# Nyström attention with a folded feed-forward: v loaded in four gated pieces, q and k in halves between sums, batch 1 loaded ahead of the weights

## Chip, cores and metric

The kernel runs on one core of one Trainium2 chip. The metric is the device time of one execution in microseconds (us), as the median of several runs. Before the change it is 294.45 us, the median of 8 runs that lie between 293.55 and 297.5.

## What is computed

```python
# attention, for each of 8 batches x 8 heads, seq 576, head_dim 64, m = 32 landmarks
q_lm = q.reshape(B, H, m, S // m, D).mean(axis=3)      # k_lm likewise
A = sm(q, k_lm);  Bm = sm(q_lm, k_lm);  C = sm(q_lm, k)
Z = Bm.T / (norm1(Bm) * norminf(Bm) + 1e-06)
for _ in range(6):
    Z = 2 * Z - Z @ Bm @ Z
attn = A @ Z @ C @ v
# feed-forward on x = attn as (4608 tokens, 512)
h = (x @ w1) * (x @ w2) @ w3
out = h @ w_out
```

`sm` is the softmax of the scaled product. w1 and w2 are 512 x 1024, w3 is 1024 x 1024, w_out is 1024 x 512, all fp32.

## The kernel before

**The algebra.** The kernel multiplies w3 and w_out once into w34 (the fold). Per batch it never forms x: it multiplies the small attention factors into w1 and w2 (tile `gt`, L403 to L419), and the large matmuls are `up` (L422), which multiplies `gt` by the normalised scores `ahat` for eight units j and both weights, and `down` (L439), which multiplies their product `ab` by w34 and stores 128 rows at a time. An even batch has four down chunks, an odd one five.

**One batch's attention** (`attention`, L178) is a generator. Each `yield` ends a step, and the main loop calls `steps(at)` to place one step between two pieces of matmul work. Step 1 turns landmark sums into the tile `lm` (L183 on TensorE, L188 on ScalarE, `qbd` on VectorE). Then come the small scores (L199), the scores of C with their partial sums on GpSimd (`presum`, L235 to L240), `bmn` and `bmbd` on GpSimd (L259, L262), the scores of A (L274), two steps `cv` that read v (L305), six Newton iterations (L369), the normalisation (L353) and four steps that make `gt` (L412, which is the first reader of w1 and w2).

**Loads of a batch.** `load_qk` (L68) issues two transfers on GpSimd's queue, k and then q, cast to fp16, into `qkn`. `turn_all` (L512) issues four DMA transposes on SP's queue, two for k and two for q, from `qkn` into `qkT`. `landmarks` (L158) adds up groups of the transposed k (t = 1) or q (t = 0) with six GpSimd operations, L166 to L175, into `parts`, which step 1 of the attention reads. `load_v` (L75) is one transfer on SP's queue. `qkn`, `qkT` and `vt` have two buffers each. Batch 0 is turned on TensorE instead (`turn_on_pe`, L94), with one copy on ScalarE and one on VectorE.

**The front** (L522 to L602). `fold` (L464) is a generator with 64 steps. Step n is three matmuls (L489) of a row block of w3 with a slice of w_out; between them it turns half blocks of w3 (L476), turn(j, 1) at step 8j and turn(j+1, 0) at step 8j+5 for j from 2 on. w3 arrives in blocks 0 to 7 on SP's queue (`load_w3`, L527) into three buffers. GpSimd's queue has k and q of batch 0, then w1 and w2 in four transfers. The order of the rest is written out by hand. Two small GpSimd copies (L572, L578) act as gates: they write one element of the buffer that a load is going to fill, and read `qkn`, so the load on SP can't start before the q or k that they read is there. After 33 fold steps the loop of L589 places attention 0 between the other fold steps, and within it the loads and landmark sums of batch 1.

**The main loop** (L607 to L636). Batch b runs its eight units of `up` and its chunks of `down`; between them are the steps of attention b+1, and at the end step 1 of attention b+2. In the same pass the transposes and v of batch b+2 are issued at the start, and after the ups q and k of batch b+3 are issued and batch b+2's landmarks are summed. Batch 0 has a schedule of its own: attention 1 begins only in its third unit, and its later downs take two steps each.

Each engine executes its instructions in the order in which the program emits them, so a queue holds everything behind an instruction that waits.

Of the kernel before, what the change touches and what calls it, by code (L numbers as in the profile page):

```python
# [7 lines left out]
FP32 = mybir.dt.float32  # L8
FP16 = mybir.dt.float16
# [4 lines left out]
B = 8  # L14
H = 8
# [10 lines left out]
NP = 96  # L26
# [5 lines left out]
def kernel(  # L32
# [11 lines left out]
    nc = tc.nc  # L44
    consts = ctx.enter_context(tc.tile_pool(name="consts", bufs=1))
    wpool = ctx.enter_context(tc.tile_pool(name="wpool", bufs=1))
    pin = ctx.enter_context(tc.tile_pool(name="pin", bufs=2))
# [5 lines left out]
    def big():  # L53
        return psp.tile([128, 2, 512], FP32, name="big", bufs=3)
# [13 lines left out]
    def load_qk(st, b):  # L68
        qkn = pin.tile([128, 2, H, 384], FP16, name="qkn")
        for t, src in ((1, k), (0, q)):  # L70
            nc.gpsimd.dma_start(out=qkn[0:NP, t, :, :],
                                in_=src[b].rearrange("h (p r) d -> p h (r d)", p=NP))
        st["qkn"] = qkn

    def load_v(st, b):  # L75
        vt = st["vt"] if "vt" in st else pin.tile([128, H, 384], FP32, name="vt")
        nc.sync.dma_start(out=vt[0:NP], in_=v[b].rearrange("h (p r) d -> p h (r d)", p=NP))
        st["vt"] = vt

    def load_weight(t, w):  # L80
        for qd in range(2):
            nc.gpsimd.dma_start(out=wup[64 * qd:64 * qd + 64, :, t, :],
                                in_=w[256 * qd:256 * qd + 256, :].rearrange("(h d) j -> d h j", d=D))
# [10 lines left out]
    def turn_on_pe(st, t, h0, copy):  # L94
        if "qkT" not in st:
            st["qkT"] = pat.tile([128, 2, H, 3, NP], FP16, name="qkT")
        ps = psp.tile([128, 2, 1024], FP16, name="big", bufs=3)
        for i in range(2):
            for n in range(6):
                nc.tensor.transpose(  # L100
                    out=ps[:, i, NP * n:NP * n + NP],
                    in_=st["qkn"][0:NP, t, h0 + 2 * i + n // 3, 128 * (n % 3):128 * (n % 3) + 128],
                    identity=ident16[0:NP, 0:NP])
        copy(out=st["qkT"][:, t, h0:h0 + 4, :, :].rearrange("p (i h) c s -> p i (h c s)", i=2),
             in_=ps[:, :, 0:6 * NP])
# [49 lines left out]
        return mask4, par, ones, eye2, iit, onesq, selc, lomask  # L155


    def landmarks(st, t, eng=nc.gpsimd):  # L158
        if "parts" not in st:
            st["parts"] = pz.tile([128, 2, 2, H, 32], FP16, name="parts")  # L160
        for h0 in ((0,) if eng is nc.gpsimd else (0, 4)):
            own, n = ("", H) if eng is nc.gpsimd else ("v", 4)
            hs = slice(h0, h0 + n)
            x = st["qkT"][:, t, hs, :, :]
            tr = pat.tile([128, n, NP], FP32, name="tr" + own, bufs=1)
            eng.tensor_tensor(out=tr, in0=x[:, :, 0, :], in1=x[:, :, 1, :], op=ALU.add)  # L166
            eng.tensor_tensor(out=tr, in0=tr, in1=x[:, :, 2, :], op=ALU.add)  # L167
            t3 = tr.rearrange("p h (l g) -> p h l g", g=3)
            o = pat.tile([128, n, 32], FP32, name="o3" + own, bufs=1)
            hi, lo = st["parts"][:, 0, t, hs, :], st["parts"][:, 1, t, hs, :]  # L170
            eng.tensor_tensor(out=o, in0=t3[:, :, :, 0], in1=t3[:, :, :, 1], op=ALU.add)
            eng.tensor_tensor(out=o, in0=o, in1=t3[:, :, :, 2], op=ALU.add)  # L172

            eng.tensor_copy(out=hi, in_=o)
            eng.tensor_tensor(out=lo, in0=o, in1=hi, op=ALU.subtract)  # L175


    def attention(st, bank=None):  # L178
# [331 lines left out]
    sts = [dict() for _ in range(B)]  # L510

    def turn_all(b):  # L512
        for t in (1, 0):
            for h0 in (0, 4):
                transposes(sts[b], t, range(h0, h0 + 4))

    def steps(g, n=1):
        for _ in range(n):
            next(g, None)
# [3 lines left out]
    with tc.tile_pool(name="pf", bufs=2) as pf:  # L523
        wof, w3f = {}, {}
        wsp = pf.tile([128, 2, 8, DM], FP16, name="wsp", bufs=1)

        def load_w3(j, cc=None, eng=nc.sync):  # L527
            if j not in w3f:
                w3f[j] = pf.tile([128, DF], FP32, name="w3f", bufs=3)
            sl = slice(0, DF) if cc is None else slice(512 * cc, 512 * cc + 512)  # L530
            eng.dma_start(out=w3f[j][:, sl], in_=moe_w3[128 * j:128 * (j + 1), sl])

        def load_wout(c, eng):
            wof[c] = pf.tile([128, DM], FP32, name="wof", bufs=6)
            eng.dma_start(out=wof[c], in_=moe_w_out[128 * c:128 * c + 128, :])

        load_w3(0, 0)
        load_wout(0, nc.scalar)
        load_wout(1, nc.sync)
        load_w3(1, 0, nc.scalar)  # L540
        load_wout(2, nc.sync)
        load_wout(3, nc.scalar)
        load_w3(0, 1)
        load_wout(4, nc.scalar)
        load_w3(1, 1)
        load_wout(5, nc.scalar)

        warm = pf.tile([128, 512], FP16, name="warm", bufs=1)
        nc.vector.memset(warm, 0.0)
        psw = big()  # L550

        def warm_up(n):
            for _ in range(n):
                nc.tensor.matmul(psw[:, 0, :], warm[:, 0:128], warm, start=True, stop=True)

        warm_up(7)

        nc.gpsimd.tensor_copy(out=gate, in_=wof[4][:, 0:1])
        load_qk(sts[0], 0)
        load_weight(0, moe_w1)  # L560
        load_weight(1, moe_w2)
        mask4, par, ones, eye2, iit, onesq, selc, lomask = constants()
        fd = fold(pf, wof, w3f, wsp, warm_up)
        steps(fd, 1)
        load_wout(6, nc.sync)
        load_wout(7, nc.sync)
        load_w3(2)
        steps(fd, 7)
        load_w3(3)
        steps(fd, 11)  # L570
        w3f[4] = pf.tile([128, DF], FP32, name="w3f", bufs=3)
        nc.gpsimd.tensor_copy(out=w3f[4][0:NP, 0:1], in_=sts[0]["qkn"][0:NP, 1, 0, 0:1])  # L572
        load_w3(4)
        turn_on_pe(sts[0], 1, 0, nc.scalar.copy)
        turn_on_pe(sts[0], 1, 4, nc.vector.tensor_copy)
        landmarks(sts[0], 1)
        sts[0]["vt"] = pin.tile([128, H, 384], FP32, name="vt")
        nc.gpsimd.tensor_copy(out=sts[0]["vt"][0:NP, 0, 0:1], in_=sts[0]["qkn"][0:NP, 0, 0, 0:1])  # L578
        load_v(sts[0], 0)
        load_qk(sts[1], 1)  # L580
        steps(fd, 5)
        turn_on_pe(sts[0], 0, 0, nc.scalar.copy)
        turn_on_pe(sts[0], 0, 4, nc.vector.tensor_copy)
        landmarks(sts[0], 0)
        steps(fd, 3)
        load_w3(5)
        steps(fd, 6)
        at = attention(sts[0])
        for n, m in enumerate((2, 2, 2, 2, 2, 2, 2, 1, 1, 1, 1, 1, 1, 1, 2, 2, 2, 2, 2, 1)):  # L589
            steps(at)  # L590
            if n == 3:
                load_w3(6)
            elif n == 7:
                load_w3(7)
                load_v(sts[1], 1)
                turn_all(1)
                landmarks(sts[1], 1)
                load_qk(sts[2], 2)
                landmarks(sts[1], 0)
            steps(fd, m)  # L600
        steps(at, 30)
        steps(fd, 64)  # L602
    pab = ctx.enter_context(tc.tile_pool(name="pab", bufs=3))
    at = attention(sts[1], acc)


    for b in range(B):  # L607
        st = sts[b]
        ab = st["ab"] = pab.tile([128, 8, S], FP16, name="ab")
        if b + 2 < B:  # L610
            turn_all(b + 2)
            load_v(sts[b + 2], b + 2)
        if b % 2 == 0:
            chunks = [[(b, ab, 128 * t, 128)] for t in range(4)]
        else:
            chunks = [[(b - 1, sts[b - 1]["ab"], 512, 64), (b, ab, 0, 64)]]
            chunks += [[(b, ab, 64 + 128 * t, 128)] for t in range(4)]
        for j in range(8):
            up(st, j, 0)
            steps(at, (0, 0, 1, 1, 1, 1, 1, 2)[j] if b == 0 else 1)  # L620
            up(st, j, 1)
        if b + 3 < B:
            load_qk(sts[b + 3], b + 3)
        if b + 2 < B:
            landmarks(sts[b + 2], 1)
            landmarks(sts[b + 2], 0)
        nxt = attention(sts[b + 2], acc) if b + 2 < B else iter(())
        hold = {}
        nd = 2 * len(chunks)
        for n in range(nd):  # L630
            bank = (lambda: big()[:, 0, :]) if n // 2 % 2 else acc
            down(chunks[n // 2], n % 2, hold, bank)
            steps(at, 2 if n == 6 and nd == 8 or b == 0 and n > 3 else 1)
        steps(at, 30)
        steps(nxt)
        at = nxt  # L636
# [30 lines left out]
```

## Time and profile before

| | |
|---|---|
| median of 8 runs | 294.45 us |
| the profiled execution's own time | 294.78 us |
| its span, first to last instruction | 292.7 us |
| TensorE (PE) busy | 276.1 us, 94% |
| VectorE (DVE) busy | 166.8 us, 57% |
| GpSimd (POOL) busy | 146.6 us, 50% |
| ScalarE (ACT) busy | 127.9 us, 44% |
| DMA | 45.56 MB, mean 156 GB/s |
| first `up` of batch 0 | 75.45 us after the start |

The page of the profile divides the span into equal slices, lists busy time per engine and the costliest groups of instructions by source line, and follows the chain of work that ended last. Further answers are taken from the trace: the waits of one engine by line and releaser, tables of busy time for chosen stretches, the instructions in order of time, and the transfers with the time from issue to landing. L12 is line 12 of the kernel before. SPq and POOLq are the instruction streams that issue transfers; PEld is TensorE's weight load. The granted clock is the share of full speed that TensorE had.

### The profile page before, as it was taken

The numbers are of one execution on the slowest core, as the hardware profiler recorded it, in microseconds if no ns is written. First come the engines' busy times: TensorE is split into PE (matmuls) and PEld (weight loads), VectorE is DVE, ScalarE is ACT, GpSimd is POOL, SyncE is SP. The second block draws the span as 40 slices with busy tenths as digits, with TensorE's granted clock in tenths as the row PEclk, the third lists the DMA queues.
The fourth block names the chain that finished last, engine by engine and source line by source line (L and its number), as shares of the span: only waits on it lengthen the run. The fifth ranks groups of instructions, "written<-read, shape, count | busy, mean of one in ns | idle before, by whom it ended". The sixth has DMA issues, their size and how long they took to land.

```text
span 292.7 us, 9468 instructions
## 1 busy us (share of the span) xinstructions
PE 276.1 (94%) x4028; PEld 151.5 (52%) x4028; DVE 166.8 (57%) x430; ACT 127.9 (44%) x207; POOL 146.6 (50%) x190
## 2 busy tenths in 40 slices
PE   8999878999999899999999999999999999999993
PEld 3456435543574366436644753376457435744741
DVE  7733223364475677647656765476666655665720
ACT  3635224224471374247426722572366246625531
POOL 1506916098069839923991698069809931500000
PEclk9999979999999999999999999999999999999999
DMA  7999999929969569947996999399959532012124
GB/s 252 282 240 243 211 271 258 155 50 175 168 148 133 142 141 163 210 140 139 167 210 173 163 206 195 79 171 215 203 127 157 129 102 72 4 36 76 37 56 123
DMA packets 61449, 45.56 MB, mean 156 GB/s; under 512 B 35040, under 2 KB 53472, under 8 KB 61408
## 3 DMA queue, kind: packets, MB, share of 16 engines
q1 hardware_dynamic: 47056, 32.12, 49.9%
q0 software_dynamic: 13632, 11.54, 25.4%
q10 hardware_dynamic: 720, 1.31, 1.3%
q8 instruction: 31, 0.51, 0.7%
q14 instruction: 10, 0.08, 0.1%
HBM read 38.80 MB, written 9.44 MB: 165 GB/s over the span
## 4 chain that ended last, share of the span: by engine, by line
PE 77%; DMA 6%; DVE 6%; ACT 6%; issue 2%; POOL 2%; SPq 0%; DVEq 0%; ACTq 0%; POOLq 0%
PE big L426 18%; PE acc L446 13%; PE big L446 11%; PE acc L489 8%; DMA w3f<-in_moe_w_dram 6%; PE big L412 6%; PE big L369 4%; DVE ab L432 4%; PE small L305 2%; ACT a_sb L430 2%; PE big L476 2%; PE acc L305 2%; PE small L489 2%; PE big L353 1%; PE big L274 1%
## 5 line engine op out<-in xcount | busy, mean ns | idle before, releaser
L426 PE MATMUL big<-ahat,gt 128*128 128x288 f16 x512 | 74.1, 286 | 2.8 <-ACT a_sb L430 1.7
L432 DVE TENSOR_TENSOR ab<-a_sb,big 128x576 f16<-128x576 f16 x64 | 48.0, 750 | 18.7 <-PE big L426 7.8
L426 PEld LDWEIGHTS <-gt 128*128 128x128 f16 x512 | 47.2, 98 | 19.3 <-issue 4.4
L430 ACT CAST a_sb<-big 128x576 f16<-128x576 f32 x64 | 40.9, 639 | 37.1 <-PE big L426 36.3
L235 POOL TENSOR_TENSOR t<-ect 96x384 f32<-96x384 f32 x16 | 15.9, 994 | 71.5 <-ACT ect L228 70.9
L489 PE MATMUL acc<-wsp,w3t 128*128 128x512 f16 x168 | 42.7, 388 | 0.5 <-ACT w L492 0.5
L446 PE MATMUL acc<-w,ab 128*128 128x512 f16 (+1 forms) x192 | 41.0, 382 | 0.1
L446 PEld LDWEIGHTS <-ab 128*128 128x128 f16 (+1 forms) x320 | 24.0, 100 | 32.7 <-issue 9.8
L446 PE MATMUL big<-w,ab 128*128 128x512 f16 x128 | 32.8, 381 | 0.2 <-DVE ahat L356 0.2
L166 POOL TENSOR_TENSOR tr<-qkT 128x768 f32<-128x768 f16 x16 | 26.3, 1643 | 12.1 <-DMA qkT<-qkn 7.2
L418 DVE TENSOR_SCALAR gt<-big 128x1024 f16<-128x1024 f32 x16 | 19.6, 1225 | 21.7 <-PE big L412 21.7
L489 PEld LDWEIGHTS <-w3t 128*128 128x128 f16 x192 | 18.0, 99 | 21.1 <-issue 4.4
L452 ACT ACTIVATE o_sb<-acc 128x512 f32<-128x512 f32 x20 | 11.9, 597 | 38.5 <-PE acc L446 36.7
L167 POOL TENSOR_TENSOR tr<-tr,qkT 128x768 f32<-128x768 f32 x16 | 26.3, 1641 | 1.3
L482 DVE SCALAR_TENSOR_TENSOR w3t<-big,w3t 128x512 f16<-128x512 f32 x16 | 11.0, 689 | 19.2 <-ACT w3t L481 19.2
L416 ACT ACTIVATE gt<-big 128x1024 f16<-128x1024 f32 x16 | 16.4, 1023 | 8.5 <-PE big L412 8.5
L412 PE MATMUL big<-wup,zt 64*32 64x512 f16 x512 | 19.3, 381 | 0.0
L452 ACT ACTIVATE o_sb<-big 128x512 f32<-128x512 f32 x16 | 9.6, 597 | 22.0 <-PE big L446 22.0
L481 ACT ACTIVATE w3t<-big 128x512 f16<-128x512 f32 x16 | 9.5, 595 | 12.5 <-PE big L476 9.4
L228 ACT ACTIVATE ect<-big 96x768 f32<-96x768 f32 x16 | 12.9, 806 | 3.6 <-PE big L224 3.1
L172 POOL TENSOR_TENSOR o<-o,tr 128x256 f32<-128x256 f32 x16 | 12.8, 799 | 1.3
L356 DVE TENSOR_TENSOR ahat<-eat,big 128x576 f16<-128x576 f16 x16 | 11.9, 748 | 1.2 <-PE big L353 1.2
(307 smaller groups left out, 355.3 us busy)
## 6 DMA issues: line engine op xcount, KB each, us to landing
vt<-in_v_dram SPq DMA_DIRECT2D x8, 1152.0 KB, 9.6
qkn<-in_k_dram POOLq DMA_DIRECT2D x8, 576.0 KB, 11.1
qkn<-in_q_dram POOLq DMA_DIRECT2D x8, 576.0 KB, 13.9
out_dram<-o_sb SPq DMA_DIRECT2D x24, 192.0 KB, 2.3
w3f<-in_moe_w_dram SPq DMA_DIRECT2D x6, 512.0 KB, 13.6
out_dram<-o_sb SPq DMA_DIRECT2D x24, 128.0 KB, 2.7
wup<-in_moe_w_dram POOLq DMA_DIRECT2D x4, 512.0 KB, 19.5
out_dram<-o_sb SPq DMA_DIRECT2D x24, 64.0 KB, 2.0
```

The source lines that it names most:

```text
L166: eng.tensor_tensor(out=tr, in0=x[:, :, 0, :], in1=x[:, :, 1, :], op=ALU.add)
L167: eng.tensor_tensor(out=tr, in0=tr, in1=x[:, :, 2, :], op=ALU.add)
L235: nc.gpsimd.tensor_tensor(out=t3[0:NP], in0=e[:, :, 0:3, :], in1=e[:, :, 3:6, :], op=ALU.add)
L412: nc.tensor.matmul(psG[32 * h:32 * h + 32, qd, :], zt[rs, i, h, :], wup[rs, h, w, fs], start=(i == 0), stop=(i == 1), tile_position=(64 * ...
L416: nc.scalar.activation(out=g[:, :, w, fs], in_=psG, func=AXF.Copy, scale=1.0 / ZS)
L418: nc.vector.tensor_scalar(out=g[:, :, w, fs], in0=psG, scalar1=1.0 / ZS, scalar2=None, op0=ALU.mult)
L426: nc.tensor.matmul(p[:, c, 0:HS], st["g"][:, qd, w, 128 * j:128 * j + 128], st["ahat"][qd][:, c, :], start=(qd == 0), stop=(qd == 1))
L430: nc.scalar.copy(out=st["a_sb"], in_=p[:, :, 0:HS])
L432: nc.vector.tensor_tensor(out=st["ab"][:, j, :].rearrange("p (c s) -> p c s", c=2), in0=st["a_sb"], in1=p[:, :, 0:HS], op=ALU.mult)
L446: nc.tensor.matmul(pso[o:o + sz, :], ab[:, j, s0:s0 + sz], w34[:, j, :], start=(j == 0), stop=(j == 7), tile_position=(0, o))
L452: nc.scalar.activation(out=o_sb, in_=pso[:, :], func=AXF.Copy, scale=1.0 / (X64 * X64))
L489: nc.tensor.matmul(psW[j][:, :], turned[j, c // 4][:, a, c % 4, :], wsp[:, b, c, :], start=(c == 0 and a + b == 0), stop=(c == 7 and a == 1))
```

## The change

The diff has three parts.

*In the main loop*, v of batch b+2 is no longer one load at the start of the pass. It becomes four pieces of two heads each, issued in units 4 to 7 on SP's queue. Each piece has a gate: a ScalarE copy of one column of the `a_sb` tile just made into the first element of the piece. q and k of batch b+3 become four transfers of four heads each, which GpSimd issues in the middle and at the end of each set of landmark sums instead of ahead of them. The sums are emitted after unit 5 instead of after unit 7.

*In the front*, q and k of batch 1 are issued on GpSimd's queue ahead of w1 and w2. k of batch 0 is turned after fold step 16 (before: 19) and q after step 21 (before: 24). The gate of v and its load come ahead of the k sums. Blocks 5 and 6 of w3 and batch 1's four transposes are emitted earlier; block 7 and v of batch 1 now follow the transposes on SP's queue. Attention 0 begins after 31 fold steps (before: 33).

*For batch 0*, step 1 of attention 1 is placed ahead of the main loop, and batch 0 then has one step per unit and per down, like the other even batches.

```diff
+    def load_v_piece(st, b, i, done):
+        if i == 0:
+            st["vt"] = pin.tile([128, H, 384], FP32, name="vt")
+        hs = slice(2 * i, 2 * i + 2)
+        nc.scalar.copy(out=st["vt"][0:NP, 2 * i, 0:1], in_=done)
+        nc.sync.dma_start(out=st["vt"][0:NP, hs],
+                          in_=v[b, hs].rearrange("h (p r) d -> p h (r d)", p=NP))
+
+    def qk_pieces(st, b):
+        st["qkn"] = pin.tile([128, 2, H, 384], FP16, name="qkn")
+        for t, src in ((1, k), (0, q)):
+            for i in range(2):
+                hs = slice(4 * i, 4 * i + 4)
+                nc.gpsimd.dma_start(out=st["qkn"][0:NP, t, hs, :],
+                                    in_=src[b, hs].rearrange("h (p r) d -> p h (r d)", p=NP))
+                yield
...
-    def landmarks(st, t, eng=nc.gpsimd):
+    def landmarks(st, t, eng=nc.gpsimd, pieces=iter(())):
...
             eng.tensor_tensor(out=tr, in0=tr, in1=x[:, :, 2, :], op=ALU.add)
+            next(pieces, None)
...
             eng.tensor_tensor(out=lo, in0=o, in1=hi, op=ALU.subtract)
+            next(pieces, None)
...
         load_qk(sts[0], 0)
+        load_qk(sts[1], 1)
         load_weight(0, moe_w1)
         load_weight(1, moe_w2)
...
-        steps(fd, 11)
+        steps(fd, 8)
         w3f[4] = pf.tile([128, DF], FP32, name="w3f", bufs=3)
         nc.gpsimd.tensor_copy(out=w3f[4][0:NP, 0:1], in_=sts[0]["qkn"][0:NP, 1, 0, 0:1])
         load_w3(4)
+        sts[0]["vt"] = pin.tile([128, H, 384], FP32, name="vt")
+        nc.gpsimd.tensor_copy(out=sts[0]["vt"][0:NP, 0, 0:1], in_=sts[0]["qkn"][0:NP, 0, 0, 0:1])
+        load_v(sts[0], 0)
         turn_on_pe(sts[0], 1, 0, nc.scalar.copy)
         turn_on_pe(sts[0], 1, 4, nc.vector.tensor_copy)
         landmarks(sts[0], 1)
-        sts[0]["vt"] = pin.tile([128, H, 384], FP32, name="vt")
-        nc.gpsimd.tensor_copy(out=sts[0]["vt"][0:NP, 0, 0:1], in_=sts[0]["qkn"][0:NP, 0, 0, 0:1])
-        load_v(sts[0], 0)
-        load_qk(sts[1], 1)
         steps(fd, 5)
         turn_on_pe(sts[0], 0, 0, nc.scalar.copy)
         turn_on_pe(sts[0], 0, 4, nc.vector.tensor_copy)
         landmarks(sts[0], 0)
-        steps(fd, 3)
         load_w3(5)
+        steps(fd, 4)
+        load_w3(6)
+        turn_all(1)
         steps(fd, 6)
         at = attention(sts[0])
         for n, m in enumerate((2, 2, 2, 2, 2, 2, 2, 1, 1, 1, 1, 1, 1, 1, 2, 2, 2, 2, 2, 1)):
             steps(at)
-            if n == 3:
-                load_w3(6)
-            elif n == 7:
+            if n == 1:
                 load_w3(7)
                 load_v(sts[1], 1)
-                turn_all(1)
+            elif n == 4:
                 landmarks(sts[1], 1)
                 load_qk(sts[2], 2)
                 landmarks(sts[1], 0)
...
     at = attention(sts[1], acc)
+    steps(at)
...
             turn_all(b + 2)
-            load_v(sts[b + 2], b + 2)
...
             up(st, j, 0)
-            steps(at, (0, 0, 1, 1, 1, 1, 1, 2)[j] if b == 0 else 1)
+            steps(at, 1)
+            if b + 2 < B and j > 3:
+                load_v_piece(sts[b + 2], b + 2, j - 4, st["a_sb"][0:NP, 0, 0:1])
             up(st, j, 1)
-        if b + 3 < B:
-            load_qk(sts[b + 3], b + 3)
-        if b + 2 < B:
-            landmarks(sts[b + 2], 1)
-            landmarks(sts[b + 2], 0)
+            if b + 2 < B and j == 5:
+                pieces = qk_pieces(sts[b + 3], b + 3) if b + 3 < B else iter(())
+                landmarks(sts[b + 2], 1, pieces=pieces)
+                landmarks(sts[b + 2], 0, pieces=pieces)
...
-            steps(at, 2 if n == 6 and nd == 8 or b == 0 and n > 3 else 1)
+            steps(at, 2 if n == 6 and nd == 8 else 1)
```

## The prediction

> **What bounds the kernel now.** I read the waits of TensorE first, then a table of stages, then the timeline of the front, and then the chain of waits. On the page PE is busy 94% of the span. All its waits for another engine or a transfer, largest first:
>
> ```profile
> PE small L183 <- POOL parts L174: 2.0, 1, 2.0
> PE big L426 <- ACT a_sb L430: 1.7, 8, 0.2
> PE big L476 <- DMA w3f<-in_moe_w_dram: 1.5, 2, 1.3
> ```
>
> The columns are us in total, times, longest. Two single waits, of 2.0 and 1.3 us, stand out, and both lie in the front, where w3 is folded with w_out. Everything later is many tiny ones. In the chain of waits the only transfer is that of w3f, 6% of the span. The stages (us, then PE, PEld, DVE, ACT and POOL busy, the granted clock, DMA share, GB/s):
>
> ```profile
> 35.39:38.10 2.71, 0.49 (x2) 0.10 (x2) 0.35 (x1) 0.00 (x0) 2.43 (x4) 0.88 1.14 222
> 38.10:44.47 6.37, 5.11 (x33) 2.18 (x33) 1.55 (x5) 1.61 (x3) 0.34 (x1) 0.78 1.13 287
> 75.45:104.28 28.83, 27.24 (x463) 15.26 (x461) 17.80 (x45) 14.03 (x24) 17.81 (x22) 1.00 0.68 135
> 133.45:160.02 26.57, 25.98 (x457) 14.83 (x457) 18.03 (x46) 13.06 (x22) 17.79 (x22) 1.00 0.99 178
> 189.79:216.41 26.62, 26.03 (x457) 14.88 (x458) 18.04 (x46) 13.07 (x22) 17.80 (x22) 1.00 0.92 177
> ```
>
> The first two rows are the front's hole: PE idles 2.22 us and then 1.26 us, and in between it runs at a reduced clock. The other three are the three even batches (0, 2, 4), which have the same work; batch 0 is 2.2 us longer. Odd batches carry one more down chunk and take 28.75 to 29.77.
>
> Why the hole is there shows in the front's timeline:
>
> ```profile
> 29.58 0.67 POOL L175 TENSOR_TENSOR parts<-o,parts 128x256 f16<-128x256 f32 x1
> 30.20 0.18 POOL L578 CAST vt<-qkn 96x1 f32<-96x1 f16 x1
> 30.32 0.82 POOL L71 DMA_DIRECT2D qkn<-in_k_dram  x1
> 30.40 0.33 SPq L77 DMA_DIRECT2D vt<-in_v_dram  x1
> 30.82 0.96 SPq L531 DMA_DIRECT2D w3f<-in_moe_w_dram  x2
> 31.12 0.78 POOL L71 DMA_DIRECT2D qkn<-in_q_dram  x1
> 31.90 1.66 POOL L166 TENSOR_TENSOR tr<-qkT 128x768 f32<-128x768 f16 x1
> ```
>
> GpSimd finishes the k sums (L175), only then makes the gate copy L578; SP, held at v (L77), only then gets to w3 blocks 5 and 6 (L531); block 5 lands 13.6 us after its issue, at 44.4. And GpSimd issues batch 1's loads (1.6 us) before the q sums (L166), for which PE waits at L183.
>
> **The front, step by step.** The k turn moves from fold step 19 to 16, the q turn from 24 to 21, attention's start from 33 to 31. One fold step is three matmuls, 0.65 us. PE reached turn(2,1) at 19.55; the k turn now stands there. It needs k, issued at 9.15 and landed 9.8 later, at 18.95: 0.6 us ahead. It ends at 20.7, and the sums start 0.95 later as before (L100's end 23.12, L166 at 24.07), at 21.7. But the v gate now stands ahead of them and needs q: 10.11 + 11.7 = 21.8, plus 0.18 is 22.0. That wait costs 0.3 us; queued behind it are only these sums. k sums take 6.18 (24.07 to 30.25), so 28.2; no load issue between; q sums 6.15, so 34.35, against 38.05 before. PE comes to L183 two fold steps (1.3) before its old 35.39, so at 34.1. The wait of 2.22 falls to about 0.2: **2.0 gained**.
>
> Clock: over 37.50 to 41.50 the granted clock was 0.58, so (1 - 0.58) x 4.0 = 1.7 us of PE work was lost. The Trainium skill (TensorE: Matmul & The Clock Gate, section Why this matters for your kernels) keeps full clock as long as no idle gap passes about 3 us. By that rule this hole, 1.96 + 0.26 idle, costs no clock and 0 is won; the row says it did cost. I take the row, since the slow stretch begins right there: **1.7 gained**.
>
> Block 5: SP now holds w3f[4] at 19.3, v at 22.0 (the gate), block 5 at about 22.5 instead of 30.82. With the same 13.6 us it lands at 36.1. PE wants it at 43.21 (end of work before the wait) - 2.0 - 1.7 + 1.02 (L248 0.33 and L224 0.69 now stand ahead of turn(5,0)) = 40.5. **1.26 gained**, with 4.4 us of cover.
>
> What else these moves push back: k and q of batch 1 (2.36 MB in HBM) now stand ahead of w1, w2 on POOL's queue. Before, the weights landed by about 35 (12.70 + 22.8) and are first read at L412, 65.95. Now batch 1 took 23.9 us in the worst of its rows beside SP's loads, so by 45.7; the weights took 14 us behind q: at worst 60, with w1, read first, by 53. L412 comes at 65.95 - 5.0 - 1.9 (two fold steps and a turn that now follow it) = 59, w2 a step later. Hidden, but thinly in the worst case. On SP, batch 1's four transposes now stand ahead of block 7. Before they followed it, waited for k and q (47.2, 55.0) and took 4.27, 3.48, 2.29 and 1.36 us to issue, 11.4 in all. If q lands between 34 and 45, block 7 is issued between 42 and 50 and lands 6 to 13.6 later: 48 to 64. PE wants it at 64.52 - 5.0 + 1.03 (L353, L412 now ahead) = 60.5. Middle 55: nothing; upper end 3 us of wait. The sums of batch 1 wait for the transposes, 52 to 56 plus 14, 66 to 70, against L183 at about 70: even.
>
> **Batch 0.** Attention 1 now starts ahead of the loop, and then gets one step per unit, as in batches 2 and 4. So batch 0 should take their 26.6 instead of 28.83; the two L183 matmuls (0.43) move in front: **1.8 gained**. Bounds: 0.7 (only the difference of the gaps, 1.6 against 0.6, less fills) and 2.2.
>
> **The steady batches.** In the built program GpSimd's arithmetic keeps its order: the two units sooner move nothing there, since presums and bmbd of the same batch are emitted before both places. Only the loads move. Four ScalarE copies (96x1) per batch, 24 in all, come between a_sb copies of units 4 to 7. Their cover:
>
> ```profile
> 142.09 0.64 ACT L430 CAST a_sb<-big 128x576 f16<-128x576 f32 x1 [0.98 <-PE big L426]
> 144.02 0.64 ACT L430 CAST a_sb<-big 128x576 f16<-128x576 f32 x1 [1.29 <-PE big L426]
> 145.59 0.64 ACT L430 CAST a_sb<-big 128x576 f16<-128x576 f32 x1 [0.93 <-PE big L426]
> ```
>
> ScalarE idles 0.93 to 1.29 us before each next a_sb, for PE. The nearest rows are GpSimd's gate, 0.18, and ScalarE's smallest copy, L203 at 0.22 to 0.26; a gate also waits for a_sb's end. Fully exposed it would be 24 x 0.26 = 6.2; within 0.9 us of idle I take 0. Its only transfer waits are for v two batches older, long landed. Behind a late gate stand the next a_sb, then DVE and PE.
>
> v comes later: last piece at a_sb of unit 7, 146.2 + 0.2; even with the whole load's 11.2 us it is there at 157.6, and L305 reads it at 166.7. q and k halves: issued 3.4 to about 15 us after bmbd instead of at once, the last at 155.3 to 156.9 (141.5 + 12.2 of sums + 1.6 to 3.2 of issue). Landing in 6 us (64.52 to 70.6) gives 162; SP wants it at the fourth transpose, 164.6. At the worst row, 13.9, the transposes slip 6 us, and the q sums still start after them. The sums end at 156.9 at most instead of 155.3; L183 comes at 158.7. The Trainium skill (DMA: Bandwidth & Descriptors, sections Measured and Anatomy of one DMA) speaks against pieces: at least 1 MiB per transfer, or bandwidth is lost, and some 2 us fixed for each; by that, 18 more transfers for v and 10 more for q and k are an estimated 56 us of queue. The rows say that a load of v took 9.6 us to land and is wanted some 25 us after issue; as PE waits for no v or qkn after 60 us, the rule prices cover, not time. I take 0; below it, up to -0.7 if the single 0.68 us issue gap at 176 is tied to v's burst.
>
> **Sum.** 2.0 + 1.7 + 1.26 + 1.8 = 6.8 us. The profiled execution took 294.78 (span 292.7 and 2.1 around it): 288.0. It lies 0.3 above the median, 294.45, so 287.7 of the median.
>
> **Rivals.**
> 1. *The front stays bound by transfers* (DMA share 1.08 to 1.14 up to 44 us, so nothing is moved faster): a block or the weights land 2 to 4 us late and the wait reappears at L476 or L412, perhaps with its slow clock. For it: the same bytes; against it: block 5 is issued 8 us sooner and has 4.4 us of cover. Time 290 to 292. Chance 0.14.
> 2. *The gates are exposed* by 0.2 each, 4.8, or batch 0 gains only 0.7 and half of the gates show: 292 to 294. Against it: the idle above. Chance 0.07.
> 3. *Slower: SP's order.* Block 7 stands behind transposes that wait for batch 1's q. From a landing after 60.5 every us counts; after 67.3 all is lost, and a long hole costs slow clock again. That needs q landed only at 52 or so: 52 + 4 + 13.6 = 69.6, 9 us late, less the 6.8: 296 to 298. For it: q of batch 1 landed at 55.0 before; against it: it was issued at 31.1 then, at about 12 now. Chance 0.06.
> 4. *What is said to be done isn't what acts:* the steady batches' edits do nothing for PE. That is in my forecast, not beside it.
>
> **Numbers.** Forecast (0.73): 286 to 290, likeliest 287.7. Range 285.8 to 291.8, which takes in most of rival 1. Half a per cent, 1.5 us, is about what can be told from no change: faster 0.87, same 0.07, slower 0.06.
>
> **What would show it.** PE's wait at L201 (old L183) under 0.3; no reduced clock after 35; no wait over 0.3 for w3f at L494 (old L476); batch 0 from its first up to batch 1's at 26.6; the start of batch 0 near 70.5; batches 1 to 7 within 0.3 us each; L84 copies at 0.18 to 0.26 without a PE wait for a_sb. Wrong, if a w3f or wup wait appears between 48 and 62, or if the even batches lengthen.

## Result and the profile after

The changed kernel takes 289.11 us, the median of 11 runs (288.07 to 291.79), beside 294.75 of 32 runs of the kernel before. The ratio is 0.982, with a 95% interval of 0.980 to 0.985: 4.4 to 5.9 us faster. (Medians here and below are of all runs; ratios leave out the runs that lie over 1.5% above the fastest of their kernel.) 287.7 was forecast. The profiled execution took 289.36, its span is 287.6 instead of 292.7, and the granted clock is 9 in all 40 slices of its page. Lines are now those of the kernel after: L183, L199, L412, L426, L476 and L489 of before are L201, L217, L430, L444, L494 and L507.

The waits of PE after, largest first (total, times, longest, in us):

```profile
PE acc L217 <- ACT lm L206: 1.7, 7, 0.3
PE big L444 <- ACT a_sb L448: 1.7, 8, 0.2
PE big L430 <- issue: 1.4, 1, 1.4
PE big L572 <- DVE warm L567: 1.2, 1, 1.2
PE acc L507 <- ACT w L510: 0.7, 3, 0.2
```

Both large waits of before are gone: of the wait for `parts` 0.14 is left, and the one wait for w3f (0.4) is for the very first block, at 4.6 us. In their place stands one single stall that was not there before, 1.4 at L430, for "issue", that is, for nothing the profile shows.

The timeline of GpSimd and SP shows why the two waits went:

```profile
21.23 0.18 POOL L594 CAST vt<-qkn 96x1 f32<-96x1 f16 x1 [2.71 <-DMA qkn<-in_q_dram]
21.68 1.64 POOL L183 TENSOR_TENSOR tr<-qkT 128x768 f32<-128x768 f16 x1 [0.26 <-DVE qkT L121]
...
27.80 1.64 POOL L183 TENSOR_TENSOR tr<-qkT 128x768 f32<-128x768 f16 x1
...
33.30 0.67 POOL L192 TENSOR_TENSOR parts<-o,parts 128x256 f16<-128x256 f32 x1
```

```profile
21.44 0.33 SPq L77 DMA_DIRECT2D vt<-in_v_dram  x1
21.87 6.78 SPq L549 DMA_DIRECT2D w3f<-in_moe_w_dram  x2
28.74 23.62 SPq L106 DMA_TRANSPOSE qkT<-qkn  x4
52.45 1.00 SPq L549 DMA_DIRECT2D w3f<-in_moe_w_dram  x1
```

The gate (L594) waits for q but costs the sums nothing (they start 0.26 after it, for the turn's copy). The two sets of sums follow each other with no load issue between, and the last ends at 33.97, with PE at L201 from 33.50. Block 5 is issued at 21.87 and lands 16.0 later, at 37.8; PE takes it at 40.43. Block 7 goes out at 52.45, behind transposes that hold SP for 23.62, and lands at 57.1; PE takes it at 60.69.

The stages, with the columns of the table of before (us; PE, PEld, DVE, ACT and POOL busy; clock, DMA share, GB/s):

```profile
35.42:41.00 5.58, 5.33 (x55) 3.38 (x54) 2.48 (x9) 2.14 (x5) 1.39 (x2) 1.00 1.15 256
72.96:100.42 27.46, 26.63 (x461) 15.12 (x459) 18.16 (x46) 14.60 (x28) 18.91 (x24) 1.00 0.63 125
100.42:129.52 29.10, 28.11 (x472) 15.52 (x473) 18.09 (x47) 14.18 (x27) 18.86 (x24) 1.00 0.92 170
129.52:156.09 26.57, 25.98 (x456) 14.83 (x457) 18.03 (x46) 13.71 (x26) 18.89 (x24) 1.00 0.95 175
156.09:184.85 28.76, 28.06 (x474) 15.45 (x474) 18.15 (x47) 14.19 (x27) 18.91 (x24) 1.00 0.90 171
```

Two rows of before that stand against these, the slow stretch and batch 3, and the stall of PE inside batch 3:

```profile
37.50:41.50 4.00, 3.74 (x18) 1.15 (x17) 0.69 (x1) 0.74 (x2) 0.54 (x1) 0.58 1.10 250
160.02:189.79 29.77, 28.40 (x472) 15.56 (x472) 18.14 (x47) 13.52 (x23) 17.84 (x22) 1.00 0.86 163
176.75 0.39 PE L369 MATMUL big<-sz__3051,tz__3049 32*32 32x96 f32 x13 [0.68 <-issue]
```

The clock is full where it was 0.58. The first up of batch 0 starts at 72.96 instead of 75.45. Batch 0 takes 27.46 instead of 28.83. Batch 2 (third batch row) is where it was, and batch 3 (last row) takes 28.76 instead of 29.77; 0.68 of that is the issue gap at 176, which is not there any more. So of the 5.1 us of span, the front gave 2.49, batch 0 1.37, batch 3 1.01, and all the rest 0.2.

### The profile page after: what moved, and what is told of

Same layout as the page of the kernel before. It is cut to its first block, busy times and chain, and to the rows that moved or that the text cites. A ratio compares the mean times of both kernels' runs of the same rounds, so it can differ in the third digit from the quotient of the medians.

```text
span 287.6 us, 9554 instructions
## 1 busy us (share of the span) xinstructions
PE 273.4 (95%) x4028; PEld 150.4 (52%) x4028; DVE 167.2 (58%) x430; ACT 131.7 (46%) x231; POOL 152.0 (53%) x200
## 4 chain that ended last, share of the span: by engine, by line
PE 79%; ACT 6%; DVE 6%; POOL 4%; issue 2%; DMA 1%; ACTq 0%; DVEq 0%; POOLq 0%
PE big L444 19%; PE acc L464 13%; PE big L464 11%; PE acc L507 9%; PE big L430 6%; DVE ab L450 4%; PE big L387 4%; PE small L323 2%; ACT a_sb L448 2%; PE acc L323 2%; PE small L507 2%; PE big L371 2%; PE big L242 1%; ACT lm L206 1%; PE big L494 1%
## 5 line engine op out<-in xcount | busy, mean ns | idle before, releaser
L444 PE MATMUL big<-ahat,gt 128*128 128x288 f16 x512 | 74.1, 286 | 2.8 <-ACT a_sb L448 1.7
L444 PEld LDWEIGHTS <-gt 128*128 128x128 f16 x512 | 47.1, 98 | 18.8 <-issue 3.9
L507 PE MATMUL acc<-wsp,w3t 128*128 128x512 f16 x168 | 41.6, 380 | 1.5 <-ACT w L510 0.7
L183 POOL TENSOR_TENSOR tr<-qkT 128x768 f32<-128x768 f16 x16 | 26.3, 1644 | 8.1 <-DMA qkT<-qkn 7.8
L507 PEld LDWEIGHTS <-w3t 128*128 128x128 f16 x192 | 17.6, 98 | 21.4 <-issue 3.2
L430 PE MATMUL big<-wup,zt 64*32 64x512 f16 x512 | 19.6, 381 | 1.4 <-issue 1.4
L470 ACT ACTIVATE o_sb<-big 128x512 f32<-128x512 f32 x16 | 9.6, 597 | 20.8 <-PE big L464 20.8
L499 ACT ACTIVATE w3t<-big 128x512 f16<-128x512 f32 x16 | 9.5, 594 | 11.2 <-PE big L494 6.3
```

Of the source, the lines that this page charges most:

```text
L430: nc.tensor.matmul(psG[32 * h:32 * h + 32, qd, :], zt[rs, i, h, :], wup[rs, h, w, fs], start=(i == 0), stop=(i == 1), tile_position=(64 * ...
L444: nc.tensor.matmul(p[:, c, 0:HS], st["g"][:, qd, w, 128 * j:128 * j + 128], st["ahat"][qd][:, c, :], start=(qd == 0), stop=(qd == 1))
L470: nc.scalar.activation(out=o_sb, in_=pso[:, :], func=AXF.Copy, scale=1.0 / (X64 * X64))
L507: nc.tensor.matmul(psW[j][:, :], turned[j, c // 4][:, a, c % 4, :], wsp[:, b, c, :], start=(c == 0 and a + b == 0), stop=(c == 7 and a == 1))
```

## Experiments

Each ran beside the kernel before on the same chip; ratios are to those runs, with 95% intervals.

**1. The front alone** (front of after, main loop and batch 0 of before).

```diff
         load_qk(sts[0], 0)
+        load_qk(sts[1], 1)
...
-            if n == 3:
-                load_w3(6)
-            elif n == 7:
+            if n == 1:
                 load_w3(7)
                 load_v(sts[1], 1)
-                turn_all(1)
+            elif n == 4:
                 landmarks(sts[1], 1)
```

> The front of the change alone (batch 1's q and k ahead of w1 and w2, earlier turns, v gate ahead of the k sums, block 7 behind the transposes); main loop and batch 0 as before. Theory (the gain is the front's hole plus batch 0's own schedule, the steady batches give nothing): no wait over 0.3 us at the landmark matmul or for w3f, no reduced clock, first up of batch 0 near 72 us, time about 4 us under before, 290.5 to 291.5. Rival (the steady batches' pieces carry a good part, through less contention): under 2.5 us of gain.

290.47 (6 runs), ratio 0.989 [0.985, 0.994]: 3.2 us, most of the 5.2 that the ratio of after makes. In its profile the first up of batch 0 starts at 70.76 instead of 75.45, 4.69 sooner; the prediction's front terms add up to 4.96. There is no issue gap at L412 here, but the one in batch 3 is still there, and larger:

```profile
PE big L369 <- issue: 1.1, 1, 1.1
```

**2. The main loop's edits alone** (v in gated pieces, q and k in halves, sums two units sooner).

```diff
-            load_v(sts[b + 2], b + 2)
...
+            if b + 2 < B and j > 3:
+                load_v_piece(sts[b + 2], b + 2, j - 4, st["a_sb"][0:NP, 0, 0:1])
...
+            if b + 2 < B and j == 5:
+                pieces = qk_pieces(sts[b + 3], b + 3) if b + 3 < B else iter(())
```

> The main loop's part alone (v in four gated pieces, q and k in halves, sums emitted after unit 5), front and batch 0's schedule as before. Theory: GpSimd's and TensorE's order is unchanged and every gate lies in ScalarE's idle time, so within 0.7 us of before; batches 2 to 5 at 26.6 and 28.8 each. Rival (pieces smooth the transfers): 1 to 2 us faster. Rival (28 more transfers, exposed gates): 2 to 5 us slower.

292.97 (22 runs), ratio 0.997 [0.994, 0.999]: about 1.0 faster, where the forecast took 0 and had a gain of 0.7 as its lower bound; the rival, 1 to 2 us through smoother transfers, came nearer. The hole and the half clock are as in before; the issue gap in batch 3 is gone, block 5's wait is 0.65 instead of 1.26 though nothing of the front was edited, and no PE wait for a_sb is added.

**3. Batch 0's schedule alone.**

```diff
     at = attention(sts[1], acc)
+    steps(at)
...
-            steps(at, (0, 0, 1, 1, 1, 1, 1, 2)[j] if b == 0 else 1)
+            steps(at, 1)
...
-            steps(at, 2 if n == 6 and nd == 8 or b == 0 and n > 3 else 1)
+            steps(at, 2 if n == 6 and nd == 8 else 1)
```

> Batch 0's schedule alone: step 1 of attention 1 ahead of the main loop and one step per unit and per down in batch 0; all else as before. Theory: batch 0 falls from 28.8 to 27.5 us and 0.4 us moves ahead of it: 0.7 to 1.2 us faster. Rival: step 1 ahead of the loop waits for batch 1's sums (they ended at 72.3 of 75.4 before), so the gain is lost: 0.

294.37 (22 runs), ratio 0.9985 [0.996, 1.001]: 0.4, with 1.2 as the upper end, not told from nothing. The term of 1.8 was too large.

**4. The hole filled.** The kernel before, with nine dummy matmuls in the hole ahead of attention 0; they compute nothing that is used.

```diff
+        psw = big()
+        warm_up(9)
         at = attention(sts[0])
```

> Before, with nine dummy 128x512 matmuls (1.9 us, they compute nothing that is used) placed just ahead of attention 0, where TensorE idled 2.2 us for the landmark sums. If the 2.2 us of idle time cause the reduced clock, it stays at 1.00 and the time falls by 1 to 1.7 us although nothing else is gained. If an idle gap under 3 us costs no clock and the slow stretch has another cause, the stretch stays and the time is within 0.4 us of before.

293.01 (19 runs), ratio 0.995 [0.992, 0.998]: 1.4 faster with more work. The stage where before had 0.58 (third number from the end: the clock):

```profile
39.00:43.00 4.00, 2.98 (x32) 1.62 (x30) 1.55 (x5) 1.06 (x3) 0.30 (x1) 1.00 1.12 321
```

PE idles 0.37 us at L183 and 1.02 at block 5, and the clock stays at 1.00. Of the 14 runs in the ratio 13 have a mean granted clock of 0.996 or more, of the 47 of before beside them only 19 (one half-clock stretch takes 0.006 off the mean). So the idling does cost clock. The rule that a gap up to about 3 us is free (the Trainium skill, TensorE: Matmul & The Clock Gate, section Why this matters for your kernels) fails here: 1.96 and 0.26 us were enough.

How much time the clock cost is less clear than the 1.4 looks. PE reaches block 5 at 41.78 instead of 43.21, 1.43 sooner, and that is the clock. But the first up can be 1.44 sooner (74.01 against 75.45) only because block 5 also landed sooner, at 42.76 instead of 44.42, though it was issued at the same time (30.74, before 30.82). And the issue gap of batch 3 is not in this profile: batch 3 is 1.0 us shorter, which is no effect of the clock in the hole.

**5. The v gate alone**, ahead of the k sums in the kernel before.

```diff
-        landmarks(sts[0], 1)
         sts[0]["vt"] = pin.tile([128, H, 384], FP32, name="vt")
         nc.gpsimd.tensor_copy(out=sts[0]["vt"][0:NP, 0, 0:1], in_=sts[0]["qkn"][0:NP, 0, 0, 0:1])
         load_v(sts[0], 0)
+        landmarks(sts[0], 1)
         load_qk(sts[1], 1)
```

> The kernel before with one edit: the gate of v and its load stand ahead of batch 0's k sums instead of behind them; batch 1's q and k stay between the sums. If the front's terms are separate, block 5's wait of 1.26 goes (it is issued near 24 instead of 30, and lands near 40 instead of 44.47, wanted at 43.2), while the stall of 2.2 at the k landmarks' sum on PE (L183) and the half clock after it stay: 1.3 us faster, 0.4%, about 293. If the transfers are short in the front whatever the order, v and block 5 now share the queues with more of the weights, block 5 still waits over 0.7, and the gain is under 0.6.

293.03 (22 runs), ratio 0.996 [0.994, 0.998]: 1.2, the 1.26 of the prediction. Its PE waits, and its stage behind the hole:

```profile
PE small L183 <- POOL parts L174: 1.8, 1, 1.8
...
PE big L476 <- DMA w3f<-in_moe_w_dram: 0.2, 1, 0.2
```

```profile
38.50:42.00 3.50, 3.50 (x18) 1.17 (x16) 1.55 (x5) 0.65 (x2) 0.00 (x0) 0.51 1.14 309
```

Block 5's wait is gone (0.2 is the first block), while the stall at L183 and the half clock (0.51) stay: the gate acts on this one term. That the size agrees so well is in part luck, since the wait itself was 1.26, 0.65, 0.27 and 1.02 in the profiles of before and of experiments 2, 3 and 4, which load block 5 in the same way.

**6. Batch 1's q and k behind both sums**, in the kernel before.

```diff
-        load_qk(sts[1], 1)
         steps(fd, 5)
         turn_on_pe(sts[0], 0, 0, nc.scalar.copy)
         turn_on_pe(sts[0], 0, 4, nc.vector.tensor_copy)
         landmarks(sts[0], 0)
+        load_qk(sts[1], 1)
```

> The kernel before with one edit: batch 1's q and k are issued behind batch 0's q sums instead of ahead of them, so that GpSimd spends no 1.6 us on their descriptors between the two sums. If the terms of the prediction's sum simply add, L183's stall falls from 2.2 to 0.6 and the half clock goes: 1.6 + 1.4 = 3.0 faster, near 291.5. The rival: L183's stall and block 5's wait lie in series, and block 5 lands near 44.5 whatever PE does, since v's gate is still behind the k sums; then what L183 gives is waited for again at block 5 (1.26 grows to 2.9 or more), and the kernel is within 0.8 of before.

291.46 (6 runs), ratio 0.988 [0.983, 0.993]: 3.6, about the 3.0 of the sum. The two waits of its hole, and where block 5 is taken:

```profile
PE small L183 <- POOL parts L174: 0.4, 1, 0.4
PE small L183 <- POOL parts L175: 0.4, 1, 0.4
```

```profile
40.99 0.66 PE L476 MATMUL big<-ident,w3f 128*128 128x128 f32 x4 [0.49 <-DMA w3f<-in_moe_w_dram]
```

The rival said that block 5 lands near 44.5 anyway. It is taken at 40.99, though its issue is where it was (31.04 against 30.82): with batch 1's transfers not yet on the queues it needs 9.9 us instead of 13.6 (11.2 to 13.6 in before and in experiments 2, 3 and 4, where they are). PE's earlier arrival is not waited for again. The first up comes at 72.41 here and at 74.05 in experiment 5: 3.04 and 1.40 sooner than before, together 4.44 of the 4.69 of the whole front.

**7 to 10. Parts of the main loop and the weights' order undone in the kernel after.** Four kernels side by side: after itself again, v whole, q and k whole, batch 1's q and k behind the weights.

> The changed kernel once more, as the base for the three beside it. Theory: 5 to 5.6 us under before. The 1.4 us issue gap of TensorE at the second gt matmul group of batch 0 (62.3 us) is a late fetch of instructions and not part of the change: it is absent or elsewhere in this profile. If it is caused by the changed front it stands at the same place again.

> The changed kernel with v of each batch in one load at the start of the pass again, without the ScalarE gates; q and k stay in halves. The main loop's part alone gave 1.0 us where I had expected none; the profiles with v whole showed an issue gap of 0.5 to 1.1 us in batch 3 three times in four, those with v in pieces none in two. If v's single burst causes it, the gap is back in batch 3 and the time is 0.5 to 1.2 us above the changed kernel. If the gates cost time, it is below the changed kernel by up to 4 us. If neither: within 0.4.

```diff
             turn_all(b + 2)
+            load_v(sts[b + 2], b + 2)
...
-            if b + 2 < B and j > 3:
-                load_v_piece(sts[b + 2], b + 2, j - 4, st["a_sb"][0:NP, 0, 0:1])
```

> The changed kernel with q and k of a batch in one load each, issued ahead of the landmark sums again; v stays in gated pieces. If the halves are what gave the main loop's 1.0 us, the time is 0.5 to 1.2 above the changed kernel; if they only cost GpSimd issue time (0.7 us each instead of 0.8 for a whole load, so 1.2 us more per batch on GpSimd, hidden), within 0.4.

```diff
-                pieces = qk_pieces(sts[b + 3], b + 3) if b + 3 < B else iter(())
-                landmarks(sts[b + 2], 1, pieces=pieces)
-                landmarks(sts[b + 2], 0, pieces=pieces)
+                if b + 3 < B:
+                    load_qk(sts[b + 3], b + 3)
+                landmarks(sts[b + 2], 1)
+                landmarks(sts[b + 2], 0)
```

> The changed kernel with q and k of batch 1 behind w1 and w2 on GpSimd's queue; all else as changed. The weights then land by 38, k and q of batch 1 by 42 to 46, the transposes are issued by 52 to 55 and block 7 lands by 57 to 60, still ahead of TensorE at 60.7. Theory (the place of batch 1's loads ahead of the weights is worth nothing by itself, since the loads are out of GpSimd's way in both): within 0.7 us of the changed kernel. Rival (the order of the two loads makes the gain): block 7 or the sums of batch 1 come late and it is 1.5 to 4 us above the changed kernel.

```diff
-        load_qk(sts[1], 1)
         load_weight(0, moe_w1)
         load_weight(1, moe_w2)
+        load_qk(sts[1], 1)
```

| kernel (6 runs each) | median | ratio to before |
|---|---|---|
| after, again | 289.33 | 0.985 [0.982, 0.988] |
| v whole | 290.39 | 0.986 [0.982, 0.990] |
| q, k whole | 288.45 | 0.982 [0.978, 0.985] |
| batch 1 behind w1, w2 | 287.90 | 0.980 [0.977, 0.984] |

All intervals overlap. The halves of q and k bring nothing that these times show. Nor do they show what the pieces of v are worth. But the profile of v whole (taken in its longest run, 293.69) has the issue gap of batch 3 back, at the place where before has it, and two more of 1.30 and 1.43 in the front:

```profile
175.75 0.39 PE L387 MATMUL big<-sz__3059,tz__3057 32*32 32x96 f32 x13 [1.57 <-issue]
```

This is what was expected if v's single burst causes the gap. Batch 1 ahead of w1 and w2 brings no time by itself; what acts is that it is not between the sums. In the last kernel's profile PE waits for `parts` again (1.46 and 0.37 at L201), because q of batch 0 comes at 23.40 instead of 21.23 and the gate holds the k sums for it; on the other hand it has no issue gap at L430, and its first up is at 72.84, against 72.96.

**11. Batch 2's q and k later**, in the kernel after.

```diff
                 landmarks(sts[1], 1)
-                load_qk(sts[2], 2)
                 landmarks(sts[1], 0)
+                load_qk(sts[2], 2)
```

> The kernel after with one edit: batch 2's q and k are issued behind both sums of batch 1 (near 66) instead of between them (58.7). PE's issue gap at the first use of w1 (1.43 in the profile of after, 0.60 in its second profile) began just as these two transfers started on the queue of GpSimd. If their burst holds up the fetch of PE's instructions, the gap is under 0.3 and the time 0.6 to 1.4 below after, near 288.2. If the gap belongs to the place in the program, or is the luck of a run, it stays within 0.3 to 1.4 and the time within 0.4 of after. The batch's transposes would start about 6 us later, near 72; its sums are wanted at 84, so nothing should wait for them.

288.67 (6 runs), ratio 0.982 [0.976, 0.987], not told from after. The gap is there as before, though those transfers now start at 65.9, behind it:

```profile
PE big L430 <- issue: 1.2, 1, 1.2
```

So their burst is not its cause.

**12. The two best put together**: q and k whole, and batch 1 behind the weights.

```diff
-        load_qk(sts[1], 1)
         load_weight(0, moe_w1)
         load_weight(1, moe_w2)
+        load_qk(sts[1], 1)
...
-                pieces = qk_pieces(sts[b + 3], b + 3) if b + 3 < B else iter(())
+                if b + 3 < B:
+                    load_qk(sts[b + 3], b + 3)
```

> The kernel after with two parts put back together: q and k loaded whole ahead of the sums, and batch 1's q and k behind w1 and w2. v keeps its gated pieces. Each alone came out below the second run of after (289.33): 288.45 and 287.90. If both gains are real and separate, they add: near 287.0. If they are the spread of a few runs, 288.0 to 289.0. The stall at L201 (1.46 + 0.37 with batch 1 behind the weights) should be there again, and the issue gap at the first use of w1 gone or below 0.4; those two would cancel, which speaks for the second answer.

290.35 (6 runs), ratio 0.984 [0.979, 0.989]: no gain over after, so the two low medians of 7 to 10 were spread. It has the gap of before again, for the reason that the gate's row shows (idle time in brackets), and a granted clock of 0.994 in two of its six runs, though not in the profiled one:

```profile
24.63 0.18 POOL L594 CAST vt<-qkn 96x1 f32<-96x1 f16 x1 [4.44 <-DMA qkn<-in_q_dram]
```

```profile
PE small L201 <- POOL parts L191: 2.2, 1, 2.2
```

No version was found that clearly beats the kernel after.

## Why the prediction was right, step by step

- **L183's stall, 2.0.** Right: 2.22 before, 0.14 after. The steps agree to some tenths: k sums from 21.68 (22.0 forecast), q sums to 33.97 (34.35). Experiment 6 gives the mechanism: without the load issue between the sums the stall is 0.8.
- **The clock, 1.7.** The row was the right guide and the rule was not (experiment 4: 1.4, with 0.5 to 2.2 in the interval, and not all of it from the clock), but the term was sized as if every run paid it, and paid it in full. Of the 80 runs of before in the ratios, 53 have a granted clock of 0.988 to 0.994 and a median of 294.24, the 27 others 294.19: no difference that these times show. In experiment 5, 13 such runs have 293.22 and the 9 others 292.24: 1.0 apart. One reading is that clock and block 5 are in series: in before a PE that comes late at block 5 waits less for it, and only when that wait is gone does the clock show. That is argued, not shown. The sum may still count both, since after removes both; it may not count either as the gain of its edit alone.
- **Block 5, 1.26.** Right (experiment 5: 1.2 [0.6, 1.9]); the close size is in part luck, as said there. It landed at 37.8, not 36.1, and was wanted at 40.43 (40.5 forecast).
- **The front's sum, 4.96.** In experiment 1 it is 4.69. In the profile of after only 2.92 of it arrives, counting L201's 0.43, which moved ahead. At the first use of w1 (59.47; 59 forecast) PE is still 4.6 ahead. Then the issue gap of 1.43 at 62.27 takes its share: the term that the prediction did not have.
- **Batch 0, 1.8.** The sign was right, the size wrong: "batch 0 should take their 26.6 instead of 28.83". The window of batch 2, 26.6, runs from one L199 to the next; batch 0's 28.83 runs from its first up, and that lies 0.89 ahead of the first L217 in after. Measured like with like it is 28.83 to 27.46, less the 0.43 moved ahead: 0.94. Or from first up to first up: 28.00 before, 26.62 after, and 26.7 in batches 2 and 4. So batch 0 did become like them, as forecast; what was too large is the 28.83 that it was taken from. Experiment 3 gives 0.4, with 0 in the interval. The lower bound in the prediction, 0.7, was the better estimate.
- **Gates, pieces and halves, 0.** Right for the gates: 24 copies of 191 ns, for which nobody waits; PE's waits for a_sb are 1.7 in total before and after. Of the estimated 56 us that the prediction drew from the Trainium skill (DMA: Bandwidth & Descriptors, sections Measured and Anatomy of one DMA) for 28 more transfers, nothing shows; the two sections measure transfers issued from GpSimd, and v's 18 go out on SP's queue. The lower bound, -0.7, is what came: the issue gap in batch 3. It is in the profiles of before and of experiments 1, 3, 5, 6 and 8, where v is one load (0.5 to 1.6 us), not in that of experiment 4, where v is one load too, and in none of seven profiles with v in pieces (2, after, 7, 9, 10, 11, 12). Experiment 8 puts back v alone and the gap is back, in one profile. So that it is tied to the single load is well supported; what it is worth in time the runs do not tell.
- **Rival 3** had its mechanism right, not its price: the transposes held SP for 23.6 us instead of 11.4, block 7 was issued at 52.45, later than the 42 to 50 of the forecast, and landed 3.6 ahead of its use. Block 5's margin was thinner still, 2.6 where 4.4 were forecast.

So the total came close partly by luck, as errors of the sum offset each other: 0.9 too much for batch 0 and 1.4 unforeseen at L430 (0.6 in the second profile of after), against 1.0 in batch 3 that was put at nothing. Together they are 1.3 of the 1.4 between 287.7 and 289.1.

**The issue gaps.** The trace names no releaser for them, but it keeps the packets of the instruction queue, 31 of 16 KB in after. In the 14 profiles PE has 15 issue gaps of 0.19 us or more, and each ends 1.3 to 1.6 us after the end of such a packet; gaps at the same matmul always follow the same packet of the row. At L430 in after the packet runs from 60.83 to 62.18 and PE goes on at 63.70. Where the gap is absent (1, 10, 12) that packet ended 1.8 to 3.2 before PE came. In batch 3 of before the packet begins at 174.04, while v's load is under way (issued 167.35, landed 175.90), and PE goes on at 176.75; in after it begins at 166.21 and ends 4.4 before PE comes. That is what a late fetch of PE's instructions would look like, and a packet's length alone (1.43 and 1.55 for two later ones without a gap) decides nothing. In experiment 4 the packet begins at 167.04; the added matmuls shift what lies in each packet, so it is no clean exception. No run moved a fetch alone, so this is strongly supported and not proved.

**Left open.** Why the packet of L430 is late: it stands in four profiles besides after (0.60 in experiment 7, 1.43 in 8, 0.33 in 9, 1.15 in 11). Nor is it settled what makes q of batch 0 late: the gate ran at 20.8 to 22.1 in the profiles with batch 1 next (1, after, 7, 8, 9, 11) and at 21.26, 23.40 and 24.63 in 5, 10 and 12, where weights follow; but weights follow in before and in 2, 3, 4 and 6 too, and there q landed at 21.1 to 21.9, in 6 at 23.4. Experiments 5 and 6 together, without the rest, were not tried.

## What to carry to other kernels

Find the one or two long waits on the bounding engine, follow each back to the instruction that stands in the way on its queue, and move that: one gate (experiment 5: 1.2) and one pair of load issues (experiment 6: 3.6) gave most of this gain, while 28 more transfers in the steady loop gave about 1.0, in the profiles largely as a stall of PE that went, not as a transfer that arrived sooner for anyone. Before adding up two waits and a slow clock, ask whether one hides behind the other, and take windows for "the same work" between the same two instructions. When a stall of the bounding engine goes, leave room in the estimate for a new one of about a microsecond where the program and, as it seems, its instruction fetches meet other traffic at a new time.

## What the runs showed of the hardware

- A half clock lasts 3.413 us in the records (from 37.48 in before, 38.57 in experiment 5). Idle time of 1.96 + 0.26 us goes with it in two thirds of the runs of before, not in all. The traces show what divides them. Every stretch of the clock's record is a whole number of 3.413 us windows, save the last, which the end cuts. In before, 2 and 5 the window just ahead of the half clock holds 2.21, 2.22 and 2.20 us without a matmul. In experiments 3 and 12 the hole, as long or longer (1.97 + 0.37 and 2.24 + 0.37), lies across a border, 1.50 and 1.09 in the two windows of 3 and 1.39 and 1.48 in those of 12, and the clock stays at 1.00. The most idle time in one window without a half clock behind it is 1.84 (experiment 10). The end of the program agrees: where the window of the last matmul holds 2.46 to 3.22 us without one (6, 8, 10), the next is at half clock, and where it holds 1.78 or less, not. So in these profiles the idle time within one window decides, and the border lies between 1.84 and 2.20 us.
- Four DMA transposes took SP 23.62 us to issue in the front of after, 11.6 in before, and 6.6 to 7.0 in experiments 6 and 12, so what stands behind a transpose on its queue has no fixed price. The first two, 8.8 and 8.9 us each, were issued while the DMA engines were at a share of 1.13 (28.74 to 46.48); that this is the reason was not tested.
- A ScalarE copy of 96x1 took 191 ns, a load issue of half of k or q on GpSimd 0.69 to 0.73 us and of a whole one 0.77 to 0.84 (but the first of all 0.97): halves nearly double the issue time, and POOL is busy 5.4 us longer in all, at no cost here.
